# Moving the input loads of an attention stage from SyncE's queue to ScalarE's, one at a time

## The chip, the cores and the metric

The kernel runs on one core of one Trainium2 chip. The metric is the time of one execution in device microseconds (us), as the median of several runs; lower is better. The five engines of the core are TensorE (PE in the profile, with PEld for its weight loads), VectorE (DVE), ScalarE (ACT), GpSimd (POOL) and SyncE (SP). SP computes nothing here, it only issues transfers. ScalarE can issue transfers too, from its own instruction stream and into its own queue. A transfer that an engine issues stands in that engine's program order: while its conditions are not met, all that follows on that engine waits.

## The reference, cut to what matters

Attention with rotary position embedding over 4 batches of 8 heads, 576 positions of 64 elements, then two dense layers with gates. The dense layers are not touched by the change.

```python
def _attn_ref(q, k, v):
    ...
    q_rot, k_rot = (rotate(q), rotate(k))
    scale = 1.0 / np.sqrt(D)
    scores = scale * np.matmul(q_rot, k_rot.transpose(0, 1, 3, 2))
    scores = scores - np.max(scores, axis=-1, keepdims=True)
    attn = np.exp(scores)
    attn = attn / (np.sum(attn, axis=-1, keepdims=True) + 1e-09)
    return np.matmul(attn, v).astype(np.float32)

def reference(**kwargs):
    ...
    attn_out = _attn_ref(**attn_kwargs)
    x = np.ascontiguousarray(attn_out.transpose(0, 2, 1, 3)).reshape(B * S, H * D)
    x = _moe_ref(x=x, **moe_kwargs)
    return _moe2_ref(x=x, **moe2_kwargs)
```

## The kernel before, in words

The attention stage takes the first 303 us of the profiled span, the dense layers the rest. Attention goes head by head: 32 heads, 16 pairs. The time of one head is a **slot** (some 9 us), numbered like the head, and a slot has ten **steps**. What is done at which step is an agenda written out by hand: `at(slot, step, fn, ...)` (L313) files a function under a place, and the main loop (L763 to L784) emits at each step the scores of the head (L566), the maxima of the head two slots later (`maxima`, L518), the values of the step five before, and whatever the agenda holds there. The emitted order is each engine's program order.

The path of one pair `pr` (heads `2*pr` and `2*pr+1`, `s0 = 2*pr`):

- **Loads.** `load` (L204) fetches keys or queries of two heads (256 KB) or values of four heads (512 KB, through `load_v`, L223, which also issues the last 64 positions, `vv`, as two transfers of 64 KB through `load_tails`, L213). From pair 5 on, k and q stand at slot `2*pr - 8`, step 3, both; the values of group `g` (pairs `2g`, `2g+1`) stand at slot `4g - 2`, step 3. So every even slot from 2 to 22 has k and q in a row on SP, and every fourth one (2, 6, 10, 14, 18, 22) k, q, v and the two `vv`; slot 26 has v and `vv` alone. These are the lines that the change touches:

```python
        for pr in range(2, NPAIR):
            slot, step = {2: (-6, 1), 3: (-1, 7), 4: (1, 7)}.get(pr, (2 * pr - 8, 3))
            at(slot, step, load, "k", 2 * pr, 2, raw_p)
            at(slot, step, load, "q", 2 * pr, 2, raw_p)
        ...
            at(4 * g - 2, 3, load_v, g)
```

- **Rotation and split.** GpSimd rotates (L362, L364, L366), TensorE transposes (L385), ScalarE and VectorE split the result into a high and a low part in a tile `hl` (L784 for the call, L389).
- **Moves.** `move` (L391) copies `hl` from SBUF to SBUF into the operand tile `W` of each head, as three transfers of 288 KB each (L397, L398, L399), at slot `s0 - 4`, step 9 for the first head of the pair, ten steps later for the second. So the moves of a first head follow the loads of the same slot on SP's queue. The maxima of that head start two slots later.
- **Row of maxima.** `max_row` (L547) puts the negated maxima of head `i` as one row into its operand: TensorE transposes at slot `i - 1`, step 1.5, VectorE casts (L554), and SP issues the row (L559 for an even head; L561 and L562 for an odd one). The scores of head `i` (L577) read it at the start of slot `i`.
- **Softmax and values.** ScalarE takes the exponentials (L584; L581 for the last, short block). The scores, the exponentials' inputs, use a ring of three PSUM banks `ps_qk`, which the transpose of `max_row` also draws from. Values: L603 to L606, from the tile `VF`, which GpSimd fills from v (L405).
- **Division.** The sums go through DRAM and back: `inverse` (L626) issues SUM to DRAM (L634), its reload (L636), the reciprocals to DRAM (L640) and a broadcast `rb` of 288 KB in two transfers (L644), all on SP.
- **Weights.** Weights of the dense layers come in blocks of 512 KB on SP (L100), a few of them during attention.

A transfer signals one of eight semaphores, which all transfers of the program, on either queue, use in turn; a transfer waits before its issue until the previous one on the same semaphore has landed. So it can wait for a transfer whose data it does not read.

Of the kernel before, what the change touches and what calls it, by code (L numbers as in the profile page):

```python
# [20 lines left out]
def attention_moe_moe_kernel(  # L21
# [15 lines left out]
    nc = tc.nc  # L37
# [148 lines left out]
    with ExitStack() as att:  # L186
        const = att.enter_context(tc.tile_pool(name="const", bufs=1))
        v_p = att.enter_context(tc.tile_pool(name="v", bufs=1))
# [6 lines left out]
        raw_p = prep.enter_context(tc.tile_pool(name="raw", bufs=2))  # L195
# [5 lines left out]
        raws = {}  # L201
        srcs = {"q": q, "k": k, "v": v}

        def load(nm, h0, n, pool):  # L204

            b, h = divmod(h0, H)
            t = raws[nm, h0 // n] = pool.tile([P, n, ST, D], F32, tag=nm, name=f"{nm}{h0}")
            nc.sync.dma_start(
                out=t.rearrange("p h t d -> p h (t d)"),
                in_=srcs[nm][b, h : h + n, 0:SM, :].rearrange("h (p t) d -> p h (t d)", t=ST),  # L210
            )

        def load_tails(names, g, pool, queue=nc.sync):  # L213

            b, h = divmod(4 * g, H)
            t = raws[names, g] = pool.tile([P, 4, D], F32, tag=names, name=f"{names}{g}")
            for j in range(2):
                queue.dma_start(
                    out=t[j * TL : (j + 1) * TL],
                    in_=srcs[names[j]][b, h : h + 4, SM:S, :].rearrange("h p d -> p h d"),  # L220
                )

        def load_v(g):  # L223
            load("v", 4 * g, 4, v_p)
            load_tails("vv", g, v_p)

        def raw(pr, nm):
# [26 lines left out]
        for j in range(2):  # L254
            nc.sync.dma_start(out=tabt[j * TL : (j + 1) * TL], in_=rope_tail[TL:P])
        load("k", 2, 2, raw_p)
        load("q", 2, 2, raw_p)
        load_v(0)

        ident = const.tile([P, P], F32, name="ident")  # L260
# [52 lines left out]
        def at(slot, step, fn, *args):  # L313
            agenda.setdefault(slot * NSTEP + step, []).append((fn, args))
# [414 lines left out]
                at(s0 - 1, (5, 7)[piece], split_v, pr, piece)  # L729
        for pr in range(2, NPAIR):  # L730
            slot, step = {2: (-6, 1), 3: (-1, 7), 4: (1, 7)}.get(pr, (2 * pr - 8, 3))
            at(slot, step, load, "k", 2 * pr, 2, raw_p)
            at(slot, step, load, "q", 2 * pr, 2, raw_p)
        for g in range(1, NHEAD // 4):
            at(*{1: (-6, 1), 2: (1, 7)}.get(g, (4 * g - 8, 4)), load_tails, "kq", g, raw_p)
            at(4 * g - 2, 3, load_v, g)
        for pr in range(NPAIR):
            *steps, first = (7, 12, 21, 22, 27, 33) if pr < NPAIR - 2 else (7, 12, 18, 18, 23, 30)
            for part, step in enumerate(steps):
# [235 lines left out]
```

## Time and profile before

| | |
|---|---|
| time, median of 3 runs | 1148.03 us (1147.63 to 1148.32) |
| time of the profiled execution | 1148.91 us |
| span of the profiled execution | 1147.1 us |
| PE busy | 1134.5 us, 99% of the span |
| DVE, ACT, POOL busy | 894.6 us (78%), 451.9 us (39%), 607.3 us (53%) |
| chain that ended last, by engine | PE 96%, DMA 2%, DVE 2% |
| transfers on SP's queue (q1) and ScalarE's (q10) | 58912 packets, 87.32 MB; 720 packets, 0.52 MB |

The span is the part of an execution that the profiler covers; the time of the execution is 1.81 us longer. PE busy is the time in which TensorE had a matmul, so the room for a change that leaves the matmuls alone is in the few gaps. The chain goes back from the last instruction to whatever released it, step by step.

### The profile page before, as it was taken

Reading aid. Unit: us, or ns where it says so; the run is one execution under the profiler, and the core shown is the slowest. Engines: PE = TensorE matmul, PEld = TensorE weight load, DVE = VectorE, ACT = ScalarE, POOL = GpSimd, SP = SyncE. Lnnn points to the kernel's source line nnn. Section 1 sums busy time; section 2 is a strip of 40 time slices with the busy share of each in tenths; the row PEclk is TensorE's granted clock in tenths of the full one; section 3 lists DMA queues with packets and bytes.
Section 4 is the critical chain, followed back from the end, with each engine's and each line's share of the span. In section 5 each row is a group of like instructions: output and inputs, shape, how many; then the busy total and the mean of one; then the engine's idle time right before and its main releaser. Section 6 shows DMA issues by size and latency. Waiting matters only on the chain.

```text
span 1147.1 us, 16900 instructions
## 1 busy us (share of the span) xinstructions
PE 1134.5 (99%) x5783; PEld 963.9 (84%) x5783; DVE 894.6 (78%) x1858; ACT 451.9 (39%) x1045; POOL 607.3 (53%) x696
## 2 busy tenths in 40 slices
PE   8999999999999999999999999999999999999998
PEld 7788888888888888888888888888888888888887
DVE  8688888878587977677676666888999999999744
ACT  6666676666744322222122213345322222222221
POOL 8857677762364544444444345766555555545321
PEclk9999999999999999999999999999999999999999
DMA  7877877665131211111111110111111111110014
GB/s 190 193 192 166 199 168 189 148 160 122 41 102 37 74 37 56 37 38 55 37 56 37 37 55 19 37 37 56 37 45 49 37 56 37 56 37 1 1 37 129
DMA packets 59718, 88.93 MB, mean 78 GB/s; under 512 B 18304, under 2 KB 31632, under 8 KB 59632
## 3 DMA queue, kind: packets, MB, share of 16 engines
q1 hardware_dynamic: 58912, 87.32, 28.8%
q8 instruction: 46, 0.75, 0.3%
q10 hardware_dynamic: 720, 0.52, 0.1%
q14 instruction: 40, 0.33, 0.1%
HBM read 55.45 MB, written 4.87 MB: 53 GB/s over the span
## 4 chain that ended last, share of the span: by engine, by line
PE 96%; DMA 2%; DVE 2%; ACT 0%; issue 0%; SPq 0%; ACTq 0%
PE h L815 14%; PE h L816 14%; PE h L814 14%; PE pv L606 10%; PE o L814 10%; PE o L815 10%; PE o L816 10%; PE s L577 7%; PE mt L531 3%; DMA W<-row 1%; PE pv L604 1%; PE pv L603 1%; DVE MX L533 1%; PE Tq L385 1%; PE Tk L385 1%; DMA W<-hl 1%
## 5 line engine op out<-in xcount | busy, mean ns | idle before, releaser
L846 POOL TENSOR_TENSOR gl<-g,gh 128x512 fp32r<-128x512 f32 (+1 forms) x140 | 169.1, 1208 | 348.0 <-ACT gh L845 240.7
L845 ACT CAST gh<-g 128x512 fp32r<-128x512 f32 (+1 forms) x140 | 81.0, 579 | 262.3 <-DVE g L835 139.4
L577 PE MATMUL s<-W 128*128 128x288 f32 (+1 forms) x640 | 180.0, 361 | 4.1 <-DMA W<-row 3.6
L815 PE MATMUL h<-xl,wh 128*128 128x512 f32 (+1 forms) x480 | 176.6, 368 | 0.0
L814 PE MATMUL h<-xh,wh 128*128 128x512 f32 (+1 forms) x480 | 176.6, 368 | 0.0
L816 PE MATMUL h<-xh,wl 128*128 128x512 f32 (+1 forms) x480 | 176.5, 368 | 0.0
L606 PE MATMUL pv<-e,VF 128*128 128x288 f32 x512 | 165.2, 405 | 0.0
L533 DVE TENSOR_REDUCE MX<-mt 128x1 f32<-128x288 f32 x288 | 127.3, 450 | 38.8 <-PE mt L531 37.1
L141 POOL TENSOR_TENSOR ca<-ca,wh 128x256 f32<-128x256 f32 x136 | 110.5, 812 | 72.4 <-DVE cm L135 51.4
L584 ACT ACTIVATE e<-s 128x288 f32<-128x288 f32 x256 | 104.9, 410 | 68.1 <-PE s L577 65.6
L136 ACT CAST wh<-ca 128x256 fp32r<-128x256 f32 x136 | 55.1, 405 | 187.5 <-DVE ca L132 187.4
L577 PEld LDWEIGHTS s<-W 128*128 128x128 f32 (+1 forms) x640 | 104.3, 179 | 28.7 <-DMA W<-row 4.6
L143 POOL TENSOR_TENSOR wl<-ca,cm 128x256 fp32r<-128x256 f32 x136 | 111.7, 822 | 17.7 <-DVE cm L138 12.2
L835 DVE TENSOR_TENSOR g<-h,g 128x512 f32<-128x512 f32 (+1 forms) x60 | 38.2, 637 | 105.8 <-PE h L816 103.2
L815 PE MATMUL h<-yl,wh 128*128 128x512 f32 (+1 forms) x320 | 117.7, 368 | 0.0
L816 PE MATMUL h<-yh,wl 128*128 128x512 f32 (+1 forms) x320 | 117.7, 368 | 0.0
L814 PE MATMUL h<-yh,wh 128*128 128x512 f32 (+1 forms) x320 | 117.7, 368 | 0.0
L814 PE MATMUL o<-wh,gh 128*128 128x512 f32 x290 | 112.6, 388 | 0.5 <-DVE z L899 0.5
L815 PE MATMUL o<-wl,gh 128*128 128x512 f32 x290 | 112.5, 388 | 0.0
L816 PE MATMUL o<-wh,gl 128*128 128x512 f32 x290 | 112.4, 387 | 0.0
L814 PEld LDWEIGHTS h<-xh,wh 128*128 128x128 f32 x480 | 90.5, 189 | 15.1
L816 PEld LDWEIGHTS h<-xh,wl 128*128 128x128 f32 x480 | 90.5, 189 | 15.0
(139 smaller groups left out, 2474.5 us busy)
## 6 DMA issues: line engine op xcount, KB each, us to landing
W<-hl SPq DMA_DIRECT2D x93, 288.0 KB
raw<-in_moe_w_out_dram SPq DMA_DIRECT2D x28, 512.0 KB
raw<-in_moe_w_in_dram SPq DMA_DIRECT2D x16, 512.0 KB
raw<-in_moe_w_gate_dram SPq DMA_DIRECT2D x12, 512.0 KB
raw<-in_moe_w_val_dram SPq DMA_DIRECT2D x12, 512.0 KB
rb<-d SPq DMA_DIRECT2D x32, 144.0 KB
v<-in_v_dram SPq DMA_DIRECT2D x8, 512.0 KB
k<-in_k_dram SPq DMA_DIRECT2D x15, 256.0 KB
```

The source lines that it names most:

```text
L136: nc.scalar.copy(h, a)
L141: nc.gpsimd.tensor_tensor(out=a, in0=a, in1=h.bitcast(F32), op=ALU.subtract)
L143: nc.gpsimd.tensor_tensor(out=l, in0=a, in1=mf, op=ALU.add)
L533: nc.vector.tensor_reduce(out=MX[pr % 2][:, a, c : c + 1], in_=m, axis=AX.X, op=ALU.max, negate=True)
L577: nc.tensor.matmul(s, lhsT=operand(i, st, t * P, n), rhs=operand(i, mv, a * HS, HS), start=st == "K1", stop=st == "K2")
L584: nc.scalar.activation(e, s, AF.Exp, scale=SCALE)
L606: nc.tensor.matmul(out_ps, lhsT=VF[par][:, ab, t], rhs=e, start=t == 0, stop=False)
L814: nc.tensor.matmul(ps, lhsT=ah, rhs=bh, start=j == 0, stop=False)
L815: nc.tensor.matmul(ps, lhsT=ah, rhs=bl, start=False, stop=False)
L816: nc.tensor.matmul(ps, lhsT=al, rhs=bh, start=False, stop=j == n - 1)
L845: nc.scalar.copy(hi, g)
L846: nc.gpsimd.tensor_tensor(out=lo, in0=g, in1=hi.bitcast(F32), op=ALU.subtract)
```

## The change

`load` and `load_v` take a queue. From pair 5 on, k stands at step 1 and q at step 6 of the same slot, where both stood at step 3, and both go to ScalarE's queue. The values of groups 1 to 7 go to ScalarE's queue at step 8 of the same slot, where they stood at step 3 on SP's. The tails `vv` move from step 3 to step 8 too, and stay on SP's queue. That is 11 k, 11 q and 7 v, 29 transfers, that leave SP's queue for ScalarE's; sizes, tiles and all other work are the same.

```diff
-        def load(nm, h0, n, pool):
+        def load(nm, h0, n, pool, queue=nc.sync):
...
-            nc.sync.dma_start(
+            queue.dma_start(
...
-        def load_v(g):
-            load("v", 4 * g, 4, v_p)
+        def load_v(g, queue=nc.sync):
+            load("v", 4 * g, 4, v_p, queue)
             load_tails("vv", g, v_p)
...
             slot, step = {2: (-6, 1), 3: (-1, 7), 4: (1, 7)}.get(pr, (2 * pr - 8, 3))
-            at(slot, step, load, "k", 2 * pr, 2, raw_p)
-            at(slot, step, load, "q", 2 * pr, 2, raw_p)
+            for nm, later in (("k", 1), ("q", 6)):
+                at(slot, step if pr < 5 else later, load, nm, 2 * pr, 2, raw_p, nc.sync if pr < 5 else nc.scalar)
...
-            at(4 * g - 2, 3, load_v, g)
+            at(4 * g - 2, 8, load_v, g, nc.scalar)
```

SP's queue in slot 22, before, from the row of head 23 to the row of head 24 (k30, q30 are keys and queries of pair 15, v24 and vv6 the values of group 6, hl13 and W10 the moves of pair 13):

```order
L561 DMA W11_165<-row23_3601 1x4x128
L562 DMA W11_165<-row23_3601 1x16x4
L640 DMA d2_9_3402<-r9_3403 128x9
L208 DMA k30_3630<-in_k_dram 128x2x256
L208 DMA q30_3632<-in_q_dram 128x2x256
L208 DMA v24_3634<-in_v_dram 128x4x256
L218 DMA vv6_3636<-in_v_dram 64x4x64 x2
L644 DMA rb9_3688<-d2_9_3402 64x576 x2
L634 DMA d2_10_3691<-SUM_91 2x576
L397 DMA W10_164<-hl13_3484 64x1152
L398 DMA W10_164<-hl13_3484 64x2x576
L399 DMA W10_164<-hl13_3484 64x2x576
```

The same stretch of SP's queue with the change:

```order
L561 DMA W11_165<-row23_3603 1x4x128
L562 DMA W11_165<-row23_3603 1x16x4
L640 DMA d2_9_3402<-r9_3403 128x9
L644 DMA rb9_3683<-d2_9_3402 64x576 x2
L634 DMA d2_10_3686<-SUM_91 2x576
L218 DMA vv6_3701<-in_v_dram 64x4x64 x2
L397 DMA W10_164<-hl13_3484 64x1152
L398 DMA W10_164<-hl13_3484 64x2x576
L399 DMA W10_164<-hl13_3484 64x2x576
```

The three large loads are gone, and the tails stand behind the broadcast and the sums, right ahead of the moves. What the moves wait for in the built program is in part unchanged: in slot 22 L398 still waits for the landing of q30 and L399 for that of v24, by the semaphores that they share, though they read neither; the row of head 24 (L559), which waited for vv6, now waits for rb9.

ScalarE in slot 22 with the change (e22_1 is the exponential of step 1, p22_9 that of the short block at step 9):

```order
L584 ACTIVATE e22_1_3585<-s22_1_3586 128x288
L208 DMA k30_3597<-in_k_dram 128x2x256
L584 ACTIVATE e22_2_3607<-s22_2_3608 128x288
L622 ACTIVATE SUM_91<-pv21_0_3521 1x288
L584 ACTIVATE e22_3_3622<-s22_3_3623 128x288
...
L584 ACTIVATE e22_6_3658<-s22_6_3659 128x288
L208 DMA q30_3668<-in_q_dram 128x2x256
L584 ACTIVATE e22_7_3674<-s22_7_3675 128x288
L784 CAST hl13_3484<-Tq1_13_3671 128x256
L584 ACTIVATE e22_8_3690<-s22_8_3691 128x288
L208 DMA v24_3699<-in_v_dram 128x4x256
L581 ACTIVATE p22_9_3705<-s22_9_3706 64x288
```

Each load now stands between two exponentials; without the three L208 rows the order is that of before.

In slot 2, the first slot that changes, SP's queue before (hl2 and W01 are the second moves of pair 2, row3 the row of head 3, k10, q10 and v4 the loads of pair 5 and group 1):

```order
L399 DMA W01_163<-hl2_542 64x2x576
L561 DMA W11_165<-row3_727 1x4x128
L562 DMA W11_165<-row3_727 1x16x4
L208 DMA k10_754<-in_k_dram 128x2x256
L208 DMA q10_756<-in_q_dram 128x2x256
L208 DMA v4_758<-in_v_dram 128x4x256
L218 DMA vv1_760<-in_v_dram 64x4x64 x2
L634 DMA d2_0_815<-SUM_91 2x576
L397 DMA W10_164<-hl3_707 64x1152
```

With the change k10 is issued on ScalarE right behind the exponential of step 1 of slot 2, q10 and v4 behind those of steps 6 and 8, so k10 no longer stands behind L399 and the row of head 3. In the built program L399 of W01 now waits for the landing of k10, and L398 of W10 for that of v4.

## Rows read from the trace of the kernel before

**Rows 1.** TensorE's waits, longest in total: line, releaser, us in total, times, longest.

```profile
PE s L577 <- DMA W<-row: 3.6, 3, 1.7
```

**Rows 2.** Timeline of TensorE, four starts of slots: start us, us, instruction, idle before.

```profile
55.86 0.37 PE L531 MATMUL mt<-W 128*128 128x288 f32 x1 [0.54 <-DMA W<-hl]
...
92.06 0.40 PE L577 MATMUL s<-W 128*128 128x288 f32 x1 [0.73 <-DMA W<-row]
...
199.80 0.40 PE L577 MATMUL s<-W 128*128 128x288 f32 x1 [1.24 <-DMA W<-row]
...
237.16 0.40 PE L577 MATMUL s<-W 128*128 128x288 f32 x1 [1.65 <-DMA W<-row]
```

**Rows 3.** Timeline of SP's queue in slots 22 and 23: issues.

```profile
222.33 0.57 SPq L640 DMA_DIRECT2D d<-r  x1
223.00 0.39 SPq L208 DMA_DIRECT2D k<-in_k_dram  x1
...
224.00 2.92 SPq L208 DMA_DIRECT2D v<-in_v_dram  x1
227.01 1.37 SPq L218 DMA_DIRECT2D vv<-in_v_dram  x2
228.47 1.20 SPq L644 DMA_DIRECT2D rb<-d  x2
229.73 0.55 SPq L634 DMA_DIRECT2D d<-SUM  x1
230.39 0.51 SPq L397 DMA_DIRECT2D W<-hl  x1
...
232.96 1.66 SPq L559 DMA_DIRECT2D W<-row  x1
```

**Rows 4.** Timeline of SP's queue, slot 6 (first row) and slot 18.

```profile
79.81 2.55 SPq L208 DMA_DIRECT2D v<-in_v_dram  x1
...
187.49 0.43 SPq L208 DMA_DIRECT2D v<-in_v_dram  x1
...
194.53 0.62 SPq L399 DMA_DIRECT2D W<-hl  x1
```

**Rows 5.** The waits of SP's own queue: us in total, times, longest.

```profile
SPq L644 <- DMA d<-r: 5.9, 5, 1.5
...
SPq L399 <- DMA v<-in_v_dram: 1.6, 2, 1.3
```

**Rows 6.** Windows: busy by engine, granted clock, DMA share, GB/s.

```profile
40.00:41.00 1.00, 1.00 (x9) 0.99 (x8) 0.56 (x1) 0.98 (x3) 1.00 (x1) 1.00 0.96 245
45.00:46.00 1.00, 1.00 (x9) 0.89 (x7) 0.72 (x3) 0.70 (x2) 0.92 (x3) 1.00 0.42 85
191.00:192.00 1.00, 1.00 (x7) 0.89 (x6) 1.00 (x5) 0.41 (x2) 1.00 (x2) 1.00 1.10 387
```

**Rows 7.** Timeline of SP's queue in slot 2.

```profile
40.47 0.93 SPq L399 DMA_DIRECT2D W<-hl  x1
...
44.36 0.54 SPq L208 DMA_DIRECT2D k<-in_k_dram  x1
```

**Rows 8.** Timeline of TensorE, first maximum of slot 3.

```profile
45.94 0.37 PE L531 MATMUL mt<-W 128*128 128x288 f32 x1
```

**Rows 9.** Timeline of ScalarE, slot 2 (first row) and the end of slot 18.

```profile
37.22 0.41 ACT L584 ACTIVATE e<-s 128x288 f32<-128x288 f32 x1 [0.64 <-PE s L577]
...
188.42 0.41 ACT L584 ACTIVATE e<-s 128x288 f32<-128x288 f32 x1 [0.21 <-PE s L577]
189.31 0.40 ACT L581 ACTIVATE p<-s 64x288 fp32r<-64x288 f32 x1 [0.47 <-PE s L577]
189.61 0.39 ACT L584 ACTIVATE s<-s 64x288 f32<-64x288 f32 x1
```

**Rows 10.** One source tile's instructions: loads of the tables on ScalarE's queue, ns min/median/max.

```profile
L244 ACTq DMA_DIRECT2D tab<-in_rope_main_dram x2: 417/429/441, 0.7 to 1.2; - x2
```

**Rows 11.** Timeline of TensorE, the transpose of the row in slot 19.

```profile
191.05 0.44 PE L552 MATMUL mr<-identr,MJ 128*128 128x128 f32 x1
```

## The prediction, made before the changed kernel was run

> **What bounds the kernel now.** I read the page first (its numbers are in the table above): TensorE is busy for 1134.5 us of a span of 1147.1 us. So only TensorE's gaps are for sale, and the next view is its waits, for who ends them. The longest is for a transfer, the row of maxima, with 3.6 us in 3 waits [rows 1]. The timeline of TensorE says where, and adds one wait for a move of the operands: 0.54 us at the start of slot 4 (the move), 0.73 us of slot 8, 1.24 us of slot 20, 1.65 us of slot 24 [rows 2]. These 4.16 us are all that a change of queues can win. Each lies two slots behind a slot whose burst on SP holds values: 2, 6, 18, 22. Even slots with keys and queries alone show none.
>
> Then SP's queue, for why the row came late. In slot 22 the load of v held SP for 2.92 us, where such an issue takes 0.43 us elsewhere [rows 3, 4]. Behind it stand the tails, the broadcast, the sums and the moves, so the moves began to issue at 230.39 and the row of head 24 at 232.96 [rows 3]. Slot 6 is alike, with 2.55 us [rows 4]. Slot 18 is another case: v was issued in 0.43 us, but L399, which waits for v's landing by a shared semaphore, went only at 194.53, 7.04 us after v's issue [rows 4], with the DMA engines full at 387 GB/s [rows 6]. The waits of SP's queue name the same wait, twice [rows 5].
>
> **The change part by part.**
>
> *Issue work on ScalarE.* ScalarE gets 29 transfers. Its queue's only loads in the trace took 0.43 us each to issue [rows 10], so 29 x 0.43 = 12.5 us of ScalarE, spread over slots 2 to 26. What hides it is ScalarE's idle time between exponentials. The tightest place is v's: the exponential of step 8 of slot 18 ended at 188.83, the next began at 189.31 after 0.47 us of waiting for TensorE [rows 9]; 0.43 fits. If it does not, the cover behind is the ring of banks: the short block's exponential ended at 190.00 [rows 9], and the transpose that draws the same bank came at 191.05 [rows 11], so 1.05 us are spare. Cost taken: 0. Bounds: 0, as nothing here can gain, and, if an issue takes the longest seen on SP, 2.92 us, 2.92 - 0.47 - 1.05 = 1.40 us for each v. The keys and queries that ScalarE refills were read by GpSimd a slot or more ahead in the agenda, so I expect no wait there; the semaphores that the 29 wait on belong to transfers of an earlier slot.
>
> *Issue work off SP.* In slot 22 the stretch from k's issue to that of the tails, 223.00 to 227.01, is freed [rows 3]. Not all of it is won. The broadcast now stands right behind the store of the reciprocals, whose issue ended at 222.90, and must wait for it to land, 1.5 us at the longest [rows 3, 5]; so it goes at about 224.4. The broadcast 1.20, the sums 0.55 and the tails 1.37 us [rows 3], with 0.2 between them, put the first move at 227.7 in place of 230.39, 2.7 us sooner, against a stall of 1.65. The tails, moved to right ahead of the moves, are counted in this.
>
> *v itself.* Its place is behind the exponential of step 8. In slot 18 that is 188.83 against 187.49, 1.34 us later [rows 4, 9]. Shifted likewise, slot 22's v issues from 225.34 to 225.77 in place of 224.00 to 226.92, so it ends 1.1 us sooner; slot 6's ends at 81.58 in place of 82.36, 0.8 sooner [rows 3, 4]. L399 still waits for v in slot 22, but with no later landing, and with the first moves ahead of it. I take both stalls as gone: 0.73 + 1.65 us. Bounds: 0.73 + 1.1 if v's landing sets the row alone, or the whole.
>
> *Slot 18.* There v is issued later and the engines are full, so only less work ahead can help. Ahead of v on SP stood a weight block, k and q; with v that is 1.5 MB, 4.1 us at 387 GB/s of the 7.04. Now k goes out in step 1, q before v, and the weights lie on the other queue. If v has the engines to itself behind q, its landing gains 2 us or more less the 1.34; if it shares them evenly with the weights, it gains nothing. Bounds 0 and 1.24; I take the middle, 0.62, since no row says how two queues share.
>
> First what the rows show of that: in slot 18 the landing, not the issue, held the move [rows 4, 6]. The Trainium skill says in "DMA: Bandwidth & Descriptors", section "Issuing engines are not separate DMA queues", that transfers of all issuing engines run on the same 16 DMA engines and interleave, and that a second issuer "will only save the time on the sequencer". By that, slot 18's 1.24 us would stay; it is a rival below.
>
> *Slot 2.* The burst that held back the moves for slot 4 goes, and with it the 0.54 us [rows 2]. But the early slots pay. k10 was issued at 44.36, behind the second moves of pair 2 and the row of head 3 [rows 7]; now it goes behind the exponential that ended at 37.63 [rows 9], into engines that are full (0.96 of their time, 245 GB/s at 40 to 41) and fall idle only in 45 to 46 (0.42, 85 GB/s) [rows 6]. Those moves are first needed at 45.94 [rows 8]. So there is some 0.4 us of slack, and k10's 256 KB are 1.07 us at 245 GB/s: a new stall of 1.07 - 0.4 = 0.67 us at the start of slot 3. L399 of these moves, issued at 40.47 [rows 7], now also waits for k10's landing. Bounds: 0, if the slack is larger, and 2.14 - 0.4 = 1.74, if q10 comes in between as well. I take 0.67, as q10 stands at step 6, late for that.
>
> *Other slots.* Where there is no stall now, k goes out two steps sooner, ahead of the row of the odd head; that row has the rest of the slot. Nothing counted. The granted clock in the windows read is 1.00, the upper level of 2.4 GHz [rows 6], and gaps of a microsecond leave it there. The dense layers start sooner by what attention gains and show no waits for transfers.
>
> **Sum:** 0.54 + 0.73 + 0.62 + 1.65 - 0.67 = 2.87 us. The profiled execution took 1148.91 us (1.81 more than its span), so it would take 1146.0. The median of the runs is 0.88 below it; from there 1148.03 - 2.87 = **1145.2 us**. With the bounds of slots 2 and 18: 0.54 + 0.73 + 1.65 - 1.74 = 1.2 us won at the least, 4.16 at the most, so 1143.9 to 1146.9.
>
> **The rivals.**
>
> *A. Only issue time is won.* The two stalls behind a held issue go (0.73 + 1.65), those of slots 4 and 20 stay, and slot 3 costs 0.67: 1.71 us won, 1146.3 us. For it: the full engines in slot 18. Against: in slot 2 the loads that stood ahead of the moves are smaller by k and q at least. The rule named above gives this.
>
> *B. The moves wait for v, not for the queue.* One of them waits for v's landing in most of these slots, and v is issued 1.34 us later where its issue was not held. Then slot 20's stall grows to 1.24 + 1.34, slot 24 keeps 1.65 - 1.1 = 0.55, slots 4 and 8 lose theirs, slot 3 costs 0.67: won 0.54 + 0.73 + 1.1 - 1.34 - 0.67 = 0.36 us, 1147.7 us. For it: L399's wait for v is in the trace [rows 5]. Against: with the weights and k on other places, v need not take 7 us again.
>
> *C. ScalarE is held.* If an issue on ScalarE's queue can be held as v's was on SP's, the exponentials behind it are late, the ring of three banks runs out, and TensorE waits at each of 7 places. It decides from an issue of 0.47 + 1.05 = 1.52 us on; at 2.92 us the price is 7 x 1.40 = 9.8 us, less the 2.87: 1155.0 us, slower. For it: two of SP's v loads took this long [rows 3, 4]. Against: both stood at the third place of a burst, and ScalarE's queue holds q at most.
>
> **How the numbers follow.** Forecast 0.62, A 0.15, B 0.13, C 0.10. The range takes in the forecast's own, A and B, with half a microsecond beyond B and a little below the full gain: 1143.6 to 1148.5; outside lie C and the ends, under 0.2. A measurement of this kernel can tell about 0.2%, 2.3 us, from no change, so faster means below 1145.7 us. That is some three quarters of the forecast and hardly any of A: 0.48. C is slower: 0.10. The rest of the forecast, A and B are the same: 0.42.
>
> **What would show it.** Right: no waits of TensorE on rows at the starts of slots 8 and 24; SP's L397 of slot 22 issued some 5.4 us behind L640, where it was 8.1; 29 issues on ScalarE of 0.4 to 0.5 us, with no new wait of TensorE on an exponential; a wait for a move or a row at the start of slot 3. Wrong: slot 20's wait kept (A) or doubled, with L399 held by v (B); issues on ScalarE of more than 1.5 us (C). The forecast fails altogether if the keys, now ahead of the odd head's row, make the starts of odd slots wait, of which nothing in the trace tells.

## The result, and the profile after

The changed kernel took **1153.82 us** (median of 14 runs, 1148.56 to 1158.43), beside 1147.57 us for the kernel before (14 runs, 1145.94 to 1148.35). The ratio is 1.0057, with a 95% interval of 1.0044 to 1.0069: **slower by 0.57%**. The forecast of 1145.2 us and its whole range, 1143.6 to 1148.5, lie below. Not only the median moved: the runs of the kernel before lie within 2.4 us, those of the changed one within 10.

The profiled execution of the changed kernel took 1152.48 us, with a span of 1150.7 us. TensorE's waits for transfers, longest in total first, the view of [rows 1]:

```profile
PE s L577 <- DMA W<-row: 5.8, 4, 3.2
```

Its timeline says where. These are all waits of TensorE for transfers from slot 3 on, the view of [rows 2] (start us, us, instruction, idle before):

```profile
49.12 0.50 PE L577 MATMUL s<-W 128*128 128x288 f32 x1 [3.23 <-DMA W<-row]
...
96.32 0.40 PE L577 MATMUL s<-W 128*128 128x288 f32 x1 [1.14 <-DMA W<-row]
...
132.40 0.40 PE L577 MATMUL s<-W 128*128 128x288 f32 x1 [0.39 <-DMA W<-row]
...
204.71 0.40 PE L577 MATMUL s<-W 128*128 128x288 f32 x1 [1.03 <-DMA W<-row]
```

| start of slot | before, us | after, us | after, a second execution, us |
|---|---|---|---|
| 3 | 0 | 3.23 | 1.53 + 0.72 |
| 4 | 0.54 | 0 | 0 |
| 8 | 0.73 | 1.14 | 1.82 |
| 12 | 0 | 0.39 | 0 |
| 20 | 1.24 | 1.03 | 0.30 + 0.69 |
| 24 | 1.65 | 0 | 0.18 |
| sum | 4.16 | 5.79 | 5.24 |

So slots 4 and 24 are mended, as forecast, slot 8 is worse, and slot 3 alone takes back more than all that was won. The waits grew by 1.63 us, the span by 3.6. Most of the rest stands in the windows behind slot 3's wait (columns as in [rows 6]: engines' busy time, granted clock, DMA share, GB/s):

```profile
48.00:49.00 1.00, 0.00 (x0) 0.00 (x0) 0.00 (x0) 0.00 (x0) 0.41 (x1) 1.00 0.36 80
49.00:50.00 1.00, 0.88 (x3) 0.88 (x4) 0.05 (x1) 0.34 (x1) 0.00 (x0) 0.64 0.94 219
50.00:51.00 1.00, 1.00 (x4) 0.71 (x4) 0.94 (x3) 0.07 (x1) 0.34 (x1) 0.50 0.70 157
51.00:52.00 1.00, 1.00 (x6) 0.86 (x5) 0.46 (x2) 0.41 (x1) 1.00 (x2) 0.50 0.11 28
52.00:53.00 1.00, 1.00 (x6) 0.86 (x5) 0.73 (x3) 0.00 (x0) 0.49 (x1) 0.66 1.00 203
53.00:54.00 1.00, 1.00 (x9) 0.84 (x8) 0.46 (x1) 0.81 (x2) 0.00 (x0) 1.00 0.96 194
```

TensorE did nothing from 48 to 49 and came back at half its clock, 0.50, the lower level of 1.2 GHz: 4 and 6 matmuls in a microsecond, and 9 once the clock is back. What the clock left out is 0.36 + 0.50 + 0.50 + 0.34 = 1.7 us (1 minus the granted clock, summed over the windows). With the 1.63 us of waits that is 3.3 of the 3.6 us.

This also explains most of the spread. Each run comes with the mean granted clock of its execution, and the 14 runs of the changed kernel roughly line up by it: 1148.56 and 1150.83 us at 1.000, 1151.24 to 1153.93 at 0.998 (4 runs), 1153.70 to 1157.47 at 0.996 (3 runs), 1158.43 at 0.993. In 101 runs of the kernel before, made later on four chips for comparison, it was 0.999 or 1.000, and 0.998 once. From the means, 0.9972 and 0.9996, the clock would be some 2.7 us of the 6.25 that the median lost; that is an estimate.

**Why the row of head 3 was late.** SP's queue in slot 2, which answers to [rows 7]:

```profile
43.43 0.59 SPq L399 DMA_DIRECT2D W<-hl  x1
44.12 0.66 SPq L561 DMA_DIRECT2D W<-row  x1
```

and ScalarE's queue:

```profile
37.37 0.39 ACTq L208 DMA_DIRECT2D k<-in_k_dram  x1
```

L399 went at 43.43, where it went at 40.47 before, and with it the row behind it is late, by 2.6 us for its larger part, L561. Before:

```profile
41.50 1.49 SPq L561 DMA_DIRECT2D W<-row  x1
```

L399 waited for k10, issued 6 us earlier. But the late issue of the row is not the whole of the loss. Below is the same L561 in two more executions, of the changed kernel and of the kernel before (e7 and e15 below), and the start of slot 3 in the first; in the second TensorE had no wait there:

```profile
42.70 0.66 SPq L561 DMA_DIRECT2D W<-row  x1
...
47.45 0.40 PE L577 MATMUL s<-W 128*128 128x288 f32 x1 [1.53 <-DMA W<-row]
```

```profile
40.84 1.80 SPq L399 DMA_DIRECT2D W<-hl  x1
42.73 0.66 SPq L561 DMA_DIRECT2D W<-row  x1
```

The row was issued at the same time in both, and with the change it came 1.5 us too late, so its way took longer. Two things differ: with the change L399, right ahead of the row, went 1.2 us later (42.02), and k10, q10 and v4 had been given to ScalarE's queue (37.38, 41.81 and 44.02). Which of them counts is what the first experiments ask. The waits of SP's own queue name the wait for k10, and three more that grew, the view of [rows 5]:

```profile
SPq L644 <- DMA d<-r: 17.8, 14, 2.2
...
SPq L399 <- DMA v<-in_v_dram: 8.0, 4, 3.0
...
SPq L399 <- DMA k<-in_k_dram: 2.8, 1, 2.8
...
SPq L640 <- DMA k<-in_k_dram: 2.5, 1, 2.5
```

**Slot 6**, where the row of head 8 comes from, shows the first and the last of these:

```profile
84.42 0.35 SPq L640 DMA_DIRECT2D d<-r  x1
86.77 1.14 SPq L644 DMA_DIRECT2D rb<-d  x2
...
90.10 0.55 SPq L397 DMA_DIRECT2D W<-hl  x1
...
92.23 1.37 SPq L559 DMA_DIRECT2D W<-row  x1
```

L640 waited 2.5 us for k14 (the keys of pair 7), then rb waited 2.0 us for L640 to land, and the moves stood behind both: 5.7 us from L640 to L397. Before, L640 had no such wait, and L397 stood 7.7 us behind it:

```profile
78.13 0.59 SPq L640 DMA_DIRECT2D d<-r  x1
...
85.82 0.51 SPq L397 DMA_DIRECT2D W<-hl  x1
```

So the change won 2.0 us there, and the wait for k14 took them back. What ScalarE paid for its new work is little; the 29 issues by tile (ns min/median/max):

```profile
L208 ACTq DMA_DIRECT2D k<-in_k_dram x11: 374/375/406, 37.4 to 224.2; - x11
L208 ACTq DMA_DIRECT2D q<-in_q_dram x11: 374/374/419, 41.8 to 228.6; - x11
L208 ACTq DMA_DIRECT2D v<-in_v_dram x7: 374/375/396, 44.0 to 266.1; - x7
```

### The profile page after: what moved, and what is told of

It is laid out like the page before. It is cut to its first block, busy times and chain, and to the rows that moved or that the text cites. A ratio compares the mean times of both kernels' runs of the same rounds, so it can differ in the third digit from the quotient of the medians.

```text
span 1150.7 us, 16852 instructions
## 1 busy us (share of the span) xinstructions
PE 1136.4 (99%) x5783; PEld 965.1 (84%) x5783; DVE 895.6 (78%) x1858; ACT 451.6 (39%) x1045; POOL 607.8 (53%) x696
## 4 chain that ended last, share of the span: by engine, by line
PE 95%; DMA 2%; DVE 2%; ACT 0%; issue 0%; SPq 0%; POOL 0%; POOLq 0%; ACTq 0%
PE h L814 14%; PE h L815 14%; PE h L816 14%; PE o L814 10%; PE o L815 10%; PE o L816 10%; PE pv L606 10%; PE s L577 7%; PE mt L531 3%; DMA W<-row 2%; DVE MX L533 1%; PE pv L604 1%; PE pv L603 1%; PE Tk L385 1%; PE Tq L385 1%; DMA rb<-d 0%
## 5 line engine op out<-in xcount | busy, mean ns | idle before, releaser
L815 PEld LDWEIGHTS h<-xl,wh 128*128 128x128 f32 x480 | 90.5, 189 | 15.0
```

The lines of the kernel that those rows point to most:

```text
L815: nc.tensor.matmul(ps, lhsT=ah, rhs=bl, start=False, stop=False)
```

## The experiments

Four theories: **T1**, moves (and in slot 6 the store L640) wait for the landing of a load with which they share a semaphore; **T2**, the early loads take engine time from the moves of slot 2; **T3**, the loads in the later slots lose time by being on ScalarE's queue; **T4**, formed after the eighth run, rb's wait for the reciprocals' store holds the moves. Ratios are to runs of the kernel before on the same chip.

| run | ratio | 95% interval |
|---|---|---|
| the change | 1.0057 | 1.0044 to 1.0069 |
| the change again (e7) | 1.0065 | 1.0043 to 1.0088 |
| slot 2 as before (e1) | 1.0008 | 1.0000 to 1.0017 |
| slot 2 alone changed (e2) | 1.0029 | 1.0016 to 1.0043 |
| the change, k10 back (e3) | 1.0017 | 1.0009 to 1.0026 |
| k10 alone moved (e4) | 1.0012 | 1.0003 to 1.0022 |
| the change, other semaphores in slot 2 (e5) | 1.0063 | 1.0047 to 1.0080 |
| e1, other semaphores in slot 6 (e8) | 1.0036 | 1.0021 to 1.0050 |
| before, v at step 0 (e6) | 1.0004 | 0.9996 to 1.0013 |
| the change, rb behind the moves (e9) | 1.0031 | 1.0019 to 1.0043 |
| e1, rb behind the moves (e10) | 1.0005 | 0.9995 to 1.0014 |
| before, rb behind the moves (e11) | 1.0014 | 1.0005 to 1.0023 |
| before, v at step 0, rb behind (e12) | 1.0009 | 1.0000 to 1.0018 |
| the change, slot 2's loads later (e13) | 1.0023 | 1.0009 to 1.0036 |
| e13, rb behind the moves (e14) | 1.0004 | 0.9995 to 1.0013 |

### Slot 2 back, and slot 2 alone

Slot 2 as before, the rest changed:

```diff
-    at(slot, step if pr < 5 else later, load, nm, 2 * pr, 2, raw_p, nc.sync if pr < 5 else nc.scalar)
+    at(slot, step if pr < 6 else later, load, nm, 2 * pr, 2, raw_p, nc.sync if pr < 6 else nc.scalar)
...
-    at(4 * g - 2, 8, load_v, g, nc.scalar)
+    at(4 * g - 2, 3 if g == 1 else 8, load_v, g, nc.sync if g == 1 else nc.scalar)
```

> The loads of slot 2 (k10, q10, v4) stand on SP at step 3 again; all later ones are on ScalarE's queue as in the change. Theory T1 (L399 of W01 is held by the landing of k10, by their shared semaphore) and theory T2 (k10, q10 and v4 take the engines' time from the moves of slot 2) both expect: no wait of TensorE at slot 3, the 0.5 us at slot 4 back, the waits at slots 8, 12 and 20 still there (some 2.6 us together), so 3.1 us of waits against 4.2 before: 1146.5 us, and runs that agree within 2.5 us. Theory T3 (the later loads on ScalarE's queue are themselves the loss) expects 1150 us or more and a spread like the change's, 10 us.

Only slot 2 changed:

```diff
-    at(slot, step if pr < 5 else later, load, nm, 2 * pr, 2, raw_p, nc.sync if pr < 5 else nc.scalar)
+    at(slot, later if pr == 5 else step, load, nm, 2 * pr, 2, raw_p, nc.scalar if pr == 5 else nc.sync)
...
-    at(4 * g - 2, 8, load_v, g, nc.scalar)
+    at(4 * g - 2, 8 if g == 1 else 3, load_v, g, nc.scalar if g == 1 else nc.sync)
```

> Only k10, q10 and v4 of slot 2 go to ScalarE's queue; all later loads stand as before. T1 and T2 expect the wait of 3.2 us at slot 3 and some 1.4 us behind it at the lower clock, the 0.54 us at slot 4 gone: 1147.6 + 4.1 = 1151.7 us in a run like the profiled one, and a median up to 1154, with runs spread over 8 us or more. T3 expects about 1147.6 us.

With slot 2 back the median is 1147.76 us and the runs lie within 4.5 us; with slot 2 alone it is 1149.87, within 7.8 us. Slot 2 is most of the loss, and without it the rest of the change gains nothing: its profile shows 4.4 us of waits, where 3.1 were expected. T3 as the main cause is out. In the profile of slot 2 alone the wait at slot 3 was 0.99 us, not the 3.2 expected: it differs from execution to execution. Nor is the clock all of the spread: one run with slot 2 alone changed took 1154.88 us at 0.999.

### k10 back, and k10 alone

```diff
-    at(slot, step if pr < 5 else later, load, nm, 2 * pr, 2, raw_p, nc.sync if pr < 5 else nc.scalar)
+    old = pr < 5 or (pr, nm) == (5, "k")
+    at(slot, step if old else later, load, nm, 2 * pr, 2, raw_p, nc.sync if old else nc.scalar)
```

> The change, with k10 alone back on SP at step 3; q10 and v4 of slot 2 stay on ScalarE's queue. No move of slot 2 waits for k10. T1 expects L399 of W01 to issue at about 40.5 us and the wait at slot 3 to be under 0.7 us; time near 1147 us. T2 expects q10 and v4 to cost the moves their share still: a wait at slot 3 of 1.5 us or more.

For k10 alone, `old = (pr, nm) != (5, "k")`, and all v as before.

> Of all loads only k10 goes to ScalarE's queue, at step 1 of slot 2. In the built program the wait for its landing now falls on L562 (the last 64 entries of row 3) and not on L399. T1 expects L399 of W01 at about 40.5 us and L562 at about 43.4 us, which it had before as well, so a wait at slot 3 of under 1 us and 1147 to 1148.5 us. T2 expects the wait at slot 3 of 1.5 to 3 us all the same, as k10's 256 KB lie in the engines as in the change.

Of the 29 loads, putting one back wins 0.4%: 1149.05 us. At the start of slot 3, with k10 back (first line) and with k10 alone moved (second; a move's wait of 0.33 us follows it):

```profile
46.31 0.40 PE L577 MATMUL s<-W 128*128 128x288 f32 x1 [0.48 <-DMA W<-row]
```

```profile
46.36 0.40 PE L577 MATMUL s<-W 128*128 128x288 f32 x1 [0.45 <-DMA W<-row]
```

In the second, it is L562, the last part of the row, that waits for k10's semaphore, and it went at 43.57 without a wait; L399 was 1.98 us in its issue. Both waits are of the size that T1 had expected; T2's 1.5 us and more did not come. But T1 has nothing for what is left. With k10 back, L399 went at 40.43, as before. With k10 alone, L399 and L561 went at 40.78 and 42.85, much as in the execution of the kernel before that is shown above. In the nine profiles with slot 2's loads as before (three of the kernel before, e1, e6, e8, e10, e11 and e12) slot 3 does not wait at all. So, as far as one execution of each tells, the bytes of q10 and v4 cost the start of slot 3 some half a microsecond, and those of k10 as much. With k10 back the time was still 0.17% above the kernel before, and k10 alone cost 0.12%, so k10 has its price of 0.4% only beside the others. The two theories had to be separated.

### Other semaphores in slot 2

A transfer of 256 bytes that nobody needs shifts which semaphore goes to whom, and leaves k10 where the change put it:

```diff
+        spare = const.tile([1, D], F32, name="spare")
...
+        def spare_load(queue):
+            queue.dma_start(out=spare, in_=v[0, 0, 0:1, :])
+        at(1, 8, spare_load, nc.sync)
```

> The whole change, and one more transfer of 256 bytes into a tile that nobody reads, on SP in slot 1, step 8. It shifts the semaphores by one, so that L399 of W01 in slot 2 waits for q8 in place of k10; k10, q10 and v4 stay where the change put them, and nearly all other waits are as in the change. T1 (the wait for k10's landing by the shared semaphore is the loss): L399 of W01 goes at 40.5 to 41 in place of 43.43, the wait at the start of slot 3 falls from 3.23 us to between 0.3 and 0.8 us, the granted clock stays at 1.00 from 49 to 53 us, and the time is 1148.5 to 1150 us. T2 (k10's bytes take the engines from the moves): the wait at the start of slot 3 stays above 2 us and the time at 1152 to 1155 us.

**T1 falls as the whole cause.** L399 (here L400, lines moved by one) no longer waited for k10, went at 41.31, and was held in its issue instead. SP, then TensorE:

```profile
41.31 2.05 SPq L400 DMA_DIRECT2D W<-hl  x1
43.45 0.67 SPq L562 DMA_DIRECT2D W<-row  x1
```

```profile
47.82 0.46 PE L578 MATMUL s<-W 128*128 128x288 f32 x1 [1.86 <-DMA W<-row]
...
98.09 0.40 PE L578 MATMUL s<-W 128*128 128x288 f32 x1 [4.19 <-DMA W<-row]
```

Slot 3 waited 1.86 us, between what the theories expected, with the clock at 0.50 behind it, and the median, 1153.77 us, is that of the change. Some 0.5 us of this is the spare transfer's own issue on SP. The hold of L399 is not k10's mark: the line of the kernel before above shows 1.80 us of it without any load on ScalarE's queue, and no wait at slot 3. The surprise is the second line: slot 8, which was not touched, waited 4.19 us, and behind it the clock fell too, as it did behind 1.78 us at slot 20:

```profile
100.00:101.00 1.00, 1.00 (x5) 0.86 (x4) 0.92 (x4) 0.00 (x0) 0.00 (x0) 0.50 0.97 196
```

This profiled execution, 1159.04 us, is the longest of the six, and the slots behind slot 3 are worse in it than in the change. The unchanged median is therefore weak evidence; what stands against T1 is slot 3's own wait, with L399 only 0.5 us later than in that execution of the kernel before.

### The change again

No edit.

> The change once more, with nothing edited. T1 says that the wait at the start of slot 3 is set by how long k10 takes to land among SP's transfers, so it differs between executions (1 to 3.5 us), the clock falls behind it only where it is long, and the time follows (1149 us where the wait is about 1 us, 1152 us and more where it is over 3 us). Rival: the wait is 3.2 us in every execution and the time differs for a reason elsewhere in the span; then the gaps of attention are as before and the rest of the span is longer.

1155.25 us (1149.22 to 1157.65, 4 runs). In this execution L399 went at 42.02, and slots 3, 8 and 20 waited as in the table at the top: the same places, other sizes. As T1 expected, the clock fell behind slot 3's 1.53 + 0.72 us (0.50 from 49 to 52), and also behind slot 8's 1.82 (0.50 from 97 to 100).

### Other semaphores in slot 6

The first experiment's kernel, with `at(5, 8, spare_load)`, so that the store L640 (here L641) does not wait for k14.

> Slot 2 as before the change, the other slots as in the change (the first experiment), and one more transfer of 256 bytes on SP in slot 5, step 8, which makes L640 of pair 1 in slot 6 wait for an older transfer in place of k14; now L562 of row 7, ahead of it on SP, waits for k14. T1 (waits for landings by shared semaphores): if L562 is held as long as L640 was, the row of head 8 stays late and slot 8 still waits 1.1 to 1.4 us; SP is in order, so the wait moves up the queue with no gain. Rival (L640's wait alone, since k14 has landed by then or the row ahead has slack): slot 8 waits under 0.5 us. The time is 1147 to 1148 us by both, as a microsecond is too little to tell.

SP's queue in slot 6, and what followed on TensorE:

```profile
80.05 0.57 SPq L563 DMA_DIRECT2D W<-row  x1
80.68 0.58 SPq L641 DMA_DIRECT2D d<-r  x1
84.82 1.13 SPq L645 DMA_DIRECT2D rb<-d  x2
```

```profile
94.65 0.61 PE L578 MATMUL s<-W 128*128 128x288 f32 x1 [3.99 <-DMA W<-row]
```

As expected by T1 the wait moved up the queue, to the row (L563, held for k14), and the store then went at 80.68. But rb came only at 84.82: the 4.5 KB of the store took over 3.5 us to land, and v8 (the values of group 2) had been issued on ScalarE at 80.60, just ahead. The row was later than in the first experiment (1.42 us of wait there), the clock fell while it lasted (0.50 from 94 to 99), and the median is higher by some 0.3%; the profiled execution is the longest of the four. This is where T4 comes from: before the change the issues of k, q, v and vv stood between L640 and rb, and whatever the landing took was covered.

### v at step 0 on SP

The kernel before with one move alone, for groups 2 to 7:

```diff
-            at(4 * g - 2, 3, load_v, g)
+            at(*((4 * g - 2, 3, load_v, g) if g == 1 else (4 * g - 2, 0, load_v, g, nc.sync)))
```

> The kernel before with one move alone: the values of groups 2 to 7 and their tails go at step 0 of the same slot in place of step 3, all on SP's queue; keys and queries and group 1 stay. T1 (what made rows late was the issue of v as the third of a burst, and its landing close ahead of the moves): v at step 0 is issued in about 0.43 us, the tables' length, and has landed before the moves; the waits of slots 8, 20 and 24 (0.73, 1.24, 1.65 us) go, slot 4 keeps 0.5: 3 to 3.6 us won, 1144 to 1145 us. Rival (any load of 512 KB holds the queue for 2.5 us wherever it stands): the row of the odd head, right behind it, is late, slots 7 and 23 wait 1 us or more, and the time is within 0.2% of before.

1148.02 us, no difference. Slot 8's wait went, slot 24's fell to 0.25 us, but slot 20 kept 0.69 + 0.72 us. v alone was issued in 1.33 us, and the two vv behind it took 2.2 to 2.3 us. The gain that was expected did not come; like the prediction, it was counted from the 4.16 us.

### rb behind the moves

```diff
-    *steps, first = (7, 12, 21, 22, 27, 33) if pr < NPAIR - 2 else (7, 12, 18, 18, 23, 30)
+    *steps, first = (7, 12, 21, 22, 29.5, 36) if pr < NPAIR - 2 else (7, 12, 18, 18, 23, 30)
```

In the whole change:

> The whole change, and the broadcast rb of pairs 0 to 13 put behind the first moves of its even slot (step 9.5 in place of step 7), the products that read it three steps later. T4 (new: rb waits for the landing of the reciprocals' store, 2 to 4 us, and the moves stand behind it on SP; before the change the issue of the loads filled that time): L397 of slot 6 goes within 3 us of L640, where it was 5.7 us with the change; the waits of slots 8 and 20 fall below 0.6 us; slot 3 keeps its 1.5 to 3.2 us; the time is 1149 to 1152 us. Rival T1 alone (L640 and L399 held by the landings of k14 and v): slots 8 and 20 keep 1 us or more each and the time stays at 1153 to 1155 us.

In the first experiment's kernel:

> Slot 2 as before the change, the other slots as in the change, and rb behind the moves as in the run above. T4 with T1 for slot 2: of the waits at slot starts only slot 4 keeps about 0.9 us, the granted clock is 1.00 throughout attention, and the time is 1144 to 1145.5 us, faster than both kernels. Rival (rb only changes places with the moves, and the rows or the products on GpSimd are late in their stead): waits for rows of over 1 us stay, 1147 to 1149 us.

In the kernel before:

> The kernel before with rb alone behind the moves, and the products three steps later; all loads on SP in their burst. T4 says that before the change the burst covers the landing that rb waits for, so rb costs the moves only its issue, 1.2 us and the gap: slot 24 goes from 1.65 to about 0.4, slot 8 from 0.73 to 0, slot 20 (held by v's landing) keeps 1.24: 1145.5 to 1147 us. Rival (the moves' place in the queue is worth nothing, since the row behind them ends last): slots 8, 20 and 24 as before, 1147 to 1148.5 us.

And with v at step 0:

> The kernel before with the values of groups 2 to 7 at step 0 (the run with v at step 0) and rb behind the moves; nothing on ScalarE's queue. T4: both of what stood ahead of the moves are gone: the waits of slots 8, 20 and 24 all go, slot 4 keeps 0.5: 1143.5 to 1145.5 us. Rival: v's transfer still shares the engines with the moves and slot 20 keeps 0.7 us or more, with 1146 to 1148 us.

In the whole change the time fell to 1150.27 us. SP's queue in slot 6:

```profile
83.36 0.34 SPq L640 DMA_DIRECT2D d<-r  x1
...
85.92 0.55 SPq L397 DMA_DIRECT2D W<-hl  x1
```

2.6 us from L640 to L397 in place of 5.7, and no wait at slot 8 in TensorE's timeline, though L640 still waited 3.0 us for k14. So taking rb, its wait and its issue, from ahead of the moves is enough there, as T4 said. That k14's wait would not have been enough to take away is not shown: e8 only moved it up the queue. Slot 20 kept 1.32 us, where T4 had said under 0.6. The edit also shifted semaphores: L399's four waits for v are gone from SP's waits, so slots 10 and 18 do not tell T1 and T4 apart.

With slot 2 back as well, TensorE's waits for transfers come to 1.6 us, with no clock under 1.00 in attention; yet 1147.06 us is within the error of the kernel before, not the 1144 to 1145.5 that was expected. In the kernel before, rb behind the moves only made it slower (1148.32 us): the burst covered its landing, and now rb delays the row behind it (in slot 6 the row went at 90.28, where it went at 88.27). With v at step 0 it brought nothing either (1147.62 us, slot 20 at 1.15).

### Slot 2's loads later, and both repairs

```diff
+                later = {"k": 7, "q": 8}[nm] if pr == 5 else later
                 at(slot, step if pr < 5 else later, load, nm, 2 * pr, 2, raw_p, nc.sync if pr < 5 else nc.scalar)
```

> The whole change, but in slot 2 k10 goes on ScalarE at step 7 and q10 at step 8 (where they stood at 1 and 6 with the change), v4 at step 8 behind them; so all three are still on ScalarE's queue, but issued behind the second moves and the row of head 3. T2 (k10's bytes meet the moves of slot 2): the wait at the start of slot 3 falls to 0.5 us or less, slot 4 waits up to 1 us, slots 8 and 20 stay as in the change (1 to 4 us and 1 to 1.8 us): 1150 to 1151.5 us. Rival (a load on ScalarE's queue costs wherever it stands in the slot): the time stays at 1153 to 1155 us.

> The run above with rb behind the first moves (step 9.5) and its products three steps later. If slot 2 (T2) and rb's wait (T4) are the whole loss, the two repairs add up: no wait at a slot start over 1.3 us, the granted clock at 1.00 throughout attention, 1146 to 1147.5 us, within 0.2% of before. If a third loss is left, 1149 us or more.

With k10 and q10 still on ScalarE's queue, but issued at 42.91 and 44.11 in place of 37.37 and 41.80, the start of slot 3 is nearly clean, and the other two places are as they were:

```profile
46.60 0.37 PE L531 MATMUL mt<-W 128*128 128x288 f32 x1 [0.46 <-DMA W<-hl]
...
92.32 0.40 PE L577 MATMUL s<-W 128*128 128x288 f32 x1 [1.47 <-DMA W<-row]
...
200.81 0.40 PE L577 MATMUL s<-W 128*128 128x288 f32 x1 [1.48 <-DMA W<-row]
```

1149.41 us, a little under what T2 had said: in slot 2 the queue did not matter, the moment did. By itself this run does not tell T1 from T2, since L399 has no k10 to wait for either. Both repairs together give 1147.38 us, level with the kernel before, all ten runs at a clock of 0.999 or 1.000. TensorE's waits there:

```profile
PE s L577 <- DMA W<-row: 1.6, 4, 0.9
```

So slot 2's early loads and rb ahead of the moves are the loss, as far as a measurement can tell, and no kernel here beats the kernel before.

### The kernel before, twice more

> The kernel before once more, with nothing edited. If the 4.16 us of waits at slots 4, 8, 20 and 24 are the kernel's own, they are there again within some 0.5 us each. Rival: the profiled execution was one of the longer ones (1148.91 us, where 34 later runs have a median of 1146.87), and this one shows 2 to 3 us of them; then there was less to win than the prediction counted.

> The kernel before a third time, for the same question: 4.16 us in the same four places, or 2 to 3 us in places that differ between executions.

TensorE's waits for rows in the second and in the third execution (1147.09 and 1148.50 us):

```profile
PE s L577 <- DMA W<-row: 2.4, 3, 1.1
```

```profile
PE s L577 <- DMA W<-row: 3.3, 4, 1.1
```

2.4 and 3.3 us in place of 4.16, mostly in the same slots (8, 20 and 24), slot 24 with 1.08 us both times in place of 1.65. The profiled execution from which the prediction counted was one of the longer ones.

## Why the prediction was wrong, point by point

- **"Slot 2": the step that failed.** It gave 0.67 us, at most 1.74; the two executions of the change measured 3.23 and 2.25, and behind both the clock fell. The mechanism was named rightly, k10's bytes among the moves of slot 2, but the term was mis-sized: it took 256 KB by the mean rate of a window and set it against a slack of 0.4 us. In its place the runs showed three things. The wait for k10's landing, which the sentence that L399 "now also waits" named without a price, held L399 for 2.8 and 1.6 us (it went 6.1 and 4.6 us behind k10's issue). The bytes on the other queue made slot 3 wait 0.45 us with k10 alone, 0.48 with q10 and v4, and 1.86 with all three where L399 did not wait for k10 (e4, e3, e5); the prediction took q10 as too late to matter and did not count v4. And the clock fell. How the 3.23 us divide between the wait and the bytes stays open.
- **"Gaps of a microsecond leave it there":** true of the waits it was said of; behind the 1.65 us of slot 24 [rows 2] the kernel before shows

```profile
237.00:238.00 1.00, 0.84 (x5) 0.79 (x5) 0.23 (x1) 0.41 (x1) 0.84 (x3) 1.00 0.89 194
```

  But the new gap was not a microsecond. The sum had no term for the clock, and that term is 1.7 us in the profiled execution and the source of most of the spread.
- **"Issue work off SP":** slot 24 went to 0 (0.18 in the second execution), as forecast. For slot 22 the sketch was nearly right: rb went 2.28 us behind the issue of L640 in place of 1.5, and L397 6.2 us behind L640, where 5.4 was predicted and 8.1 [rows 3] was before:

```profile
227.46 0.58 SPq L640 DMA_DIRECT2D d<-r  x1
230.32 1.14 SPq L644 DMA_DIRECT2D rb<-d  x2
...
233.64 0.56 SPq L397 DMA_DIRECT2D W<-hl  x1
```

- **"v itself", slot 8's 0.73 as gone: wrong**, 1.14 and 1.82 us. Slot 22 was carried over to slot 6, where the store first waited for k14 and then landed late. The bound of 1.5 us on rb's wait came from [rows 5], and those waits are not of the slots with loads (there rb stood idle for 0.1 us) but of late ones where k and q no longer stood ahead of it, such as slot 28 of the kernel before, with no load of k, q or v on the way:

```profile
276.76 0.57 SPq L640 DMA_DIRECT2D d<-r  x1
278.51 1.12 SPq L644 DMA_DIRECT2D rb<-d  x2
```

  With loads on the other queue the wait was up to 2.2 us, and 3.5 and 3.9 in e8 and e5.
- **"Slot 18":** 0.62 us to remain, 1.03 and 0.99 measured. The move did wait for v, 3.0 us at the longest, and in slot 18 went 7.65 us behind v's issue (201.27 and 193.62), where it was 7.04 [rows 4]: v took as long again, with k in step 1 and the weights on the other queue. So rival B's mechanism is real in slots 10 and 18; what it costs alone no run shows. The Trainium skill says in "DMA: Bandwidth & Descriptors", section "Issuing engines are not separate DMA queues", that transfers of all issuing engines run on the same 16 DMA engines and interleave. This trace agrees: of the 1.24 us that by this were to stay, 1.03 and 0.99 did.
- **"Issue work on ScalarE", 0:** right. 0.37 to 0.42 us for each, no new wait of TensorE on an exponential; rival C, the only one on the slower side, is out. So the forecast's tenth for a slower kernel rested on the wrong cause, and no rival foresaw this one.
- **The sum:** it started from 4.16 us of waits in one execution. Two others show 2.4 and 3.3, so even a flawless change had 0.2 to 0.3% to win.

Open is why the two repairs overlap: slot 2 alone wins back 0.49%, rb alone 0.26 to 0.34%, both together 0.53%. The clock may be a part of it: its mean was 0.9972 in the change, 0.9995 with slot 2 back and 0.9988 with rb behind the moves. Open too is why e10 and e12, with waits of 1.6 and 1.7 us, fewer than any profile of the kernel before, are not faster than it. The sizes of the waits differ between executions, and single profiles don't settle it. Not tried was the full change with L399's wait for v in slot 18 taken away and nothing else.

## What to carry to other kernels

Where loads leave a burst on a queue, ask what the burst covered: a store that must land before the next transfer on that queue goes out may turn into a wait. Place a load by when its bytes move and what needs the engines then; taking it off a queue does not take it off the engines. And take the room for a gain from several executions before you spend it: here one profile showed nearly twice what another did.

## What the runs showed of the hardware

- A gap on TensorE can cost more than itself: behind 3.23 us of idle time the granted clock was 0.50 for two full windows and 0.64 and 0.66 at their sides, behind 4.19 us alike. Length alone does not tell: in e9 a wait of 2.11 us at 49.20 was followed by windows at 1.00, in the change again 1.82 us at 96.25 by windows at 0.50. Each fall cost the same: 1.70 or 1.71 us of clock in all six of the change (one), the change again (two) and e5 (three), and twice that in e8, part of it while TensorE stood still. By that, the run at 0.993 had four or five of them, which is an estimate.
- The same 256 KB load, k10, was issued at 37.37 us with slot 2 alone changed, at 37.38 and 37.37 in two executions of the change; L399, which waited for it, went at 41.46, 42.02 and 43.43 us.
- An issue on SP can be held, and by different amounts in the same program: L399 of slot 2 took 0.93, 1.80 and 0.60 us in three executions of the kernel before.
- A store of 4.5 KB needed over 3.5 us to land behind a load of 512 KB that the other queue had just been given (e8); with no load of k, q or v on the way, the transfer that waits for it went 1.2 us behind its issue (slot 28 of the kernel before).
